# A feed-forward activation by one shifted square, with phases, start and final branch placed anew

## The chip, the cores and the metric

The kernel runs on one core of a Trainium2 chip. The core has a matrix engine (TensorE, PE in the profile), three engines for elementwise work (VectorE is DVE, ScalarE is ACT, GpSimd is POOL) and a sync engine (SP) that here issues most DMAs. Each engine works through its own list of instructions in order and waits on semaphores for the others. The metric is device time in microseconds of one execution, and the median of several runs is compared. Before the change it is 707.75 us (three runs, 701.27 to 708.39).

## The reference

Two parts stand one behind the other. The first is a linear attention with a decaying state, on 4 batches of 8 heads, 768 tokens and head width 48. Its output, 3072 tokens by 384, goes through a feed-forward layer of width 2048:

```python
for t in range(S):                                   # S = 768
    y[:, :, t] = einsum('bhd,bhde->bhe', rt, state + u * kt (x) vt)
    state = wt[..., None] * state + kt (x) vt
x = y.transpose(0, 2, 1, 3).reshape(B * S, H * D)    # 3072 x 384
h = x @ w_in                                         # 3072 x 2048
g = h - np.tanh(h)
return g @ w_out                                     # 3072 x 384
```

The change is in `g = h - tanh(h)`. For small h the difference of two nearly equal numbers is computed by a series in s = h*h: g = h * s * polynomial(s).

## The kernel before

The 768 tokens of each batch are cut in two, so there are 8 blocks of 384 tokens. The attention of a block uses 64-token chunks. Block 0's attention is computed at the start by itself (`boot`). After that, one loop runs over the blocks: it does the feed-forward layer of block i in 16 steps f (128 of the 2048 columns each), and between the steps it places pieces of the attention of block i+1 ("phases", "before") and of block i+2 ("ahead"). Block 0 also loads the 16 tiles of weights and converts them from their 64-bit form with three ACT and two DVE instructions each.

One step of the feed-forward layer is six PE instructions in source (three matmuls for `hp`, three for `acc`) and an elementwise part:

```python
def first(xT, f, ps):
    hp = ps.tile([P, NB], F32, name="hp", tag="hp")          # this PSUM tile has one buffer
    for kc in reversed(range(KC)):                           # KC = 3
        nc.tensor.matmul(hp, lhsT=w_in_sb[:, f, kc, :], rhs=xT[kc], ...)
    made = nc.scalar.activation(out=h, in_=hp, func=AF.Copy, scale=1.0 / UPSCALE)
    nc.scalar.activation(out=s, in_=h, func=AF.Square)
    nc.scalar.activation(out=qa, in_=s, func=AF.Square, bias=shift[:, 0:1])
    nc.scalar.activation(out=qb, in_=s, func=AF.Square, bias=shift[:, 1:2])
    nc.scalar.activation(out=th, in_=h, func=AF.Tanh)
    nc.scalar.activation(out=big, in_=s, func=AF.Relu, bias=shift[:, 2:3])
    return g, [
        product(hs, h, SERIES, s, ALU.mult),                 # DVE, one step later
        lambda: nc.vector.tensor_tensor(out=th, in0=h, in1=th, op=ALU.subtract),
        product(hs, qa, QUAD[0][1], hs, ALU.add),
        product(g, qb, QUAD[1][1], hs, ALU.add),
        lambda: nc.vector.copy_predicated(out=g, mask=big.bitcast(I32), data=th)], made
```

So each step has six ACT and five DVE instructions on 128x384 fp32. Both forms of g are computed, and where s is above 0.25 the form with tanh is taken.

The loop (cut):

```python
for f in range(NF):                                          # NF = 16
    g, next_rest, made = first(here, f, ps_d)
    waiting.append((second, f, g))
    if f not in urgent:
        finish(rest, extra)            # the DVE part of step f-1, and DVE part of a conversion
    for name in before.get(f, ()): later.prepare(name)
    if f in phases: later.phase(ps_a, phases[f])
    for name in ahead.get(f, ()): after.prepare(name)
    ...                                # loads, conversion of weights (ACT part)
    if len(waiting) > LAG:             # LAG = 3: the second matmul of step f-3
        s, fs, gs = waiting.pop(0)
        s.add(fs, gs)                  # after step 15: ACT copies o<-acc, and the output DMA
    if later and phases.get(f) == "result 1": later.phase(ps_a, "result 2")
```

The tables of where the pieces stand, for blocks from 1 on:

```python
steps = (6, 7, 8, 9, 12)               # own, earlier, turn, update, result 1
before = {0: ("before 0",), 1: ("times_behind 2", "times_behind 0", "times_u"),
          2: ("inverse", "held"), 3: ("times_before",), 4: ("bounds",), 7: ("over",)}
ahead = {13: ("behind 2",), 14: ("behind 0",), 15: ("before 2",)}
```

`before` and `behind` are running products along the tokens (DVE scans), `times_behind`, `times_before` and `over` are products of whole tiles on DVE, `times_u` is four ACT instructions (k times u, in place of k), `bounds` two ACT instructions of 128x1560. `own`, `earlier`, `turn`, `update` and `result` are PE matmuls on 48- or 64-row pieces with copies behind them. `over` writes the tile r that the matmuls of `earlier` read.

The end: the kernel has counted whether all its assumptions hold, and branches to a general version of everything where they do not.

```python
count = ...                            # DVE, before the last g
sure = matmul(count, ones); again = (sure != expected)
for s, fs, gs in waiting: s.add(fs, gs)
with tc.If(nc.values_load(again, min_val=0, max_val=1) > 0):
    ...                                # the general version; not entered with these inputs
```

## Time and profile before

| | |
|---|---|
| median of three runs | 707.75 us |
| profiled span | 707.0 us |
| PE busy | 618.7 us (88%) |
| DVE busy | 518.2 us (73%) |
| ACT busy | 508.4 us (72%) |
| POOL busy | 7.8 us (1%) |
| DMA, mean | 61 GB/s |
| chain that ended last: PE, ACT, DVE | 49%, 22%, 21% |

Times are in us unless marked ns. A row of the timeline is: start, length, engine, line of the source, operation, output<-inputs, shape, count, and in brackets the idle time before it with what ended that wait. The trace has two records per fp32 matmul of this kind, so the three matmuls for `hp` or `acc` of a step show as x6. A row of the table of stages gives, for a stretch of time, the busy time of each engine with its number of instructions, the granted PE clock as a share of full speed, and the DMA's share and rate.

### The profile page before, as it was taken

The page shows a single profiled execution, that of the slowest core. Times are in us where ns is not written, and L with a number is a line of the kernel's source. Part 1 is how long each engine was busy: PE and PEld are TensorE (multiplying, and loading weights), DVE is VectorE, ACT ScalarE, POOL GpSimd, SP SyncE. Part 2 cuts the span into 40 slices and gives each one's busy share as a digit, 9 for nine tenths or more (in the row PEclk, how much of TensorE's full clock was granted, in tenths as well). Part 3 has the DMA queues.
Part 4 walks back from the last instruction along what each step waited for, and adds up shares of the span by engine and source line. Part 5 has one row for each costly group of instructions (what it writes and reads, how often), then busy time and mean ns, then how long its engine had stood idle before and what let it go on. Part 6 is the DMA issues. An engine that isn't in the chain of part 4 may idle for free.

```text
span 707.0 us, 13685 instructions
## 1 busy us (share of the span) xinstructions
PE 618.7 (88%) x5410; PEld 379.5 (54%) x5410; DVE 518.2 (73%) x987; ACT 508.4 (72%) x958; POOL 7.8 (1%) x38
## 2 busy tenths in 40 slices
PE   3547788988999879998899879998899898999995
PEld 3523455544665456655566446654566455665553
DVE  7677598887588876696677866687776876757672
ACT  1399999987467855779377884679467884678873
POOL 3000000000000000000000000000000000000000
PEclk9998899999899989999899998999899998999998
DMA  8174234321110212003020211102120110000001
GB/s 301 48 275 136 85 129 136 99 67 46 47 46 9 68 48 77 23 4 110 24 68 9 67 47 46 50 5 68 47 90 10 27 42 1 2 10 33 1 0 39
DMA packets 23432, 43.13 MB, mean 61 GB/s; under 512 B 2112, under 2 KB 21312, under 8 KB 23360
## 3 DMA queue, kind: packets, MB, share of 16 engines
q1 hardware_dynamic: 22944, 41.89, 18.2%
q8 instruction: 44, 0.72, 0.4%
q10 hardware_dynamic: 352, 0.25, 0.1%
q14 instruction: 28, 0.23, 0.1%
q0 software_dynamic: 64, 0.05, 0.0%
HBM read 36.28 MB, written 4.72 MB: 58 GB/s over the span
## 4 chain that ended last, share of the span: by engine, by line
PE 49%; ACT 22%; DVE 21%; issue 4%; DMA 2%; SPq 0%; DVEq 0%; ACTq 0%; PEldq 0%; PEld 0%
PE acc L599 20%; PE hp L562 20%; PE att L348 4%; DVE hs L579 4%; DVE pre L266 3%; DVE gT L587 3%; ACT h L569 3%; ACT qb L572 3%; DVE gT L579 3%; ACT s L570 2%; DVE th L584 2%; ACT k L312 2%; ACT th L573 2%; ACT junk L319 2%; DVE r L305 2%
## 5 line engine op out<-in xcount | busy, mean ns | idle before, releaser
L562 PE MATMUL hp<-xT,w_sb 128*128 128x384 f32 x768 | 279.6, 501 | 37.2 <-ACT h L569 27.4
L599 PE MATMUL acc<-w_sb,gT 128*128 128x384 f32 x768 | 284.0, 508 | 4.8 <-ACT o L604 4.0
L562 PEld LDWEIGHTS hp<-xT,w_sb 128*128 128x128 f32 x768 | 147.4, 195 | 149.2 <-ACT h L569 44.0
L599 PEld LDWEIGHTS acc<-w_sb,gT 128*128 128x128 f32 x768 | 148.2, 198 | 107.4 <-issue 10.5
L569 ACT ACTIVATE h<-hp 128x384 f32<-128x384 f32 x128 | 62.1, 485 | 130.8 <-PE hp L562 130.8
L584 DVE TENSOR_TENSOR th<-h,th 128x384 f32<-128x384 f32 x128 | 71.1, 555 | 61.3 <-ACT th L573 61.3
L579 DVE SCALAR_TENSOR_TENSOR hs<-h,s 128x384 f32<-128x384 f32 x128 | 70.3, 549 | 45.8 <-ACT s L570 45.8
L587 DVE COPY_PREDICATED gT<-big,th 128x384 f32<-128x384 int32 x128 | 76.0, 594 | 11.9
L571 ACT ACTIVATE qa<-s,shift 128x384 f32<-128x384 f32 x128 | 78.7, 615 | 4.2
L579 DVE SCALAR_TENSOR_TENSOR gT<-qb,hs 128x384 f32<-128x384 f32 x128 | 71.4, 558 | 10.7
L574 ACT ACTIVATE big<-s,shift 128x384 f32<-128x384 f32 x128 | 76.8, 600 | 0.0
L572 ACT ACTIVATE qb<-s,shift 128x384 f32<-128x384 f32 x128 | 76.7, 599 | 0.0
L579 DVE SCALAR_TENSOR_TENSOR hs<-qa,hs 128x384 f32<-128x384 f32 x128 | 70.6, 551 | 0.0
L570 ACT ACTIVATE s<-h 128x384 f32<-128x384 f32 x128 | 67.0, 523 | 4.0
L573 ACT ACTIVATE th<-h 128x384 f32<-128x384 f32 x128 | 64.9, 507 | 0.0
L355 DVE COPY_PREDICATED scores<-mask_all,att 128x768 f32<-128x768 uint8 x32 | 31.5, 1010 | 16.6 <-PE att L348 16.5
L348 PE MATMUL att<-r,post 48*64 48x64 f32 x768 | 21.8, 302 | 22.3 <-DVE r L305 22.3
L399 DVE SCALAR_TENSOR_TENSOR states<-states,pre,att 128x48 f32<-128x48 f32 x176 | 31.6, 257 | 12.6 <-PE att L388 12.6
L348 PEld LDWEIGHTS att<-r,post 48*64 48x64 f32 x768 | 20.3, 210 | 27.1 <-issue 24.2
L312 ACT ACTIVATE k<-k,u_sb 128x384 f32<-128x384 f32 x32 | 17.2, 603 | 21.6 <-DVE post L291 21.6
L277 DVE TENSOR_TENSOR_SCAN post<-w,seed 128x780 f32<-128x780 f32 x16 | 28.3, 1777 | 0.0
L266 DVE TENSOR_TENSOR_SCAN pre<-w,seed 128x780 f32<-128x780 f32 x16 | 28.2, 1767 | 0.0
(55 smaller groups left out, 334.3 us busy)
## 6 DMA issues: line engine op xcount, KB each, us to landing
raw<-in_weights SPq DMA_DIRECT2D x16, 768.0 KB, 4.3
w<-in_wT SPq DMA_DIRECT2D x7, 780.0 KB, 4.5
k<-in_kT SPq DMA_DIRECT2D x7, 768.0 KB, 4.4
r<-in_rT SPq DMA_DIRECT2D x7, 768.0 KB, 4.5
v_sb<-in_v SPq DMA_DIRECT2D x8, 576.0 KB, 3.9
out_y<-o SPq DMA_DIRECT2D x23, 192.0 KB, 2.0
xT<-late SPq DMA_DIRECT2D x44, 24.0 KB, 1.9
w<-in_wT SPq DMA_DIRECT2D x2, 390.0 KB, 5.3
```

The source lines that it names most:

```text
L348: nc.tensor.matmul(dst, lhsT=self.chunk(lhs, p, 2 * c + par)[rows], rhs=src, start=True, stop=True)
L562: nc.tensor.matmul(hp, lhsT=w_in_sb[:, f, kc, :], rhs=xT[kc], start=(kc == KC - 1), stop=(kc == 0))
L569: made = nc.scalar.activation(out=h, in_=hp, func=AF.Copy, scale=1.0 / UPSCALE)
L570: nc.scalar.activation(out=s, in_=h, func=AF.Square)
L571: nc.scalar.activation(out=qa, in_=s, func=AF.Square, bias=shift[:, 0:1])
L572: nc.scalar.activation(out=qb, in_=s, func=AF.Square, bias=shift[:, 1:2])
L573: nc.scalar.activation(out=th, in_=h, func=AF.Tanh)
L574: nc.scalar.activation(out=big, in_=s, func=AF.Relu, bias=shift[:, 2:3])
L579: return lambda: nc.vector.scalar_tensor_tensor(out=out, in0=in0, scalar=scalar, in1=in1, op0=op0, op1=ALU.mult)
L584: lambda: nc.vector.tensor_tensor(out=th, in0=h, in1=th, op=ALU.subtract),
L587: lambda: nc.vector.copy_predicated(out=g, mask=big.bitcast(I32), data=th)], made
L599: nc.tensor.matmul(acc, lhsT=g[:, j * P:(j + 1) * P], rhs=w_out_sb[:, f, :], start=(f == 0), stop=(f == NF - 1))
```

## The change

The new activation takes s = h*h once, and one shifted square: g = (( s + SHIFT )^2 + REST) * (TOP * h * s). It holds where all h*h are at most 1/64. The DVE instruction that makes s also keeps the largest s of each row, and these maxima join the count that decides on the general version. So tanh, the second shifted square, the mask and the select leave the main path. They stay in the general version (`any_h`). The square itself moves from ACT to DVE.

```diff
+SLIGHT = 2.0 ** -6
+TOP, SHIFT, REST = 0.053459249436855316, -1.2470279932022095, 4.680200099945068
...
+    def slight(h, n):
+        s, qa = (dense.tile([P, NB], F32, name=name, tag=name) for name in ("s", "qa"))
+        ...
+        def squares():
+            nc.vector.tensor_tensor_reduce(out=s, in0=h, in1=h, scale=1.0, scalar=0.0, op0=ALU.mult,
+                                           op1=ALU.max, accum_out=top[:, n:n + 1])
+            nc.scalar.activation(out=qa, in_=s, func=AF.Square, bias=shift[:, 4:5])
+        return g, squares, [product(hs, h, TOP, s, ALU.mult), product(g, qa, REST, hs, ALU.add)]
```

The pieces of the attention stand at other steps, in one table for all blocks, and `bounds` is cut in two:

```diff
-            steps = (6, 7, 8, 9, 12)
-            before = {0: ("before 0",), 1: ("times_behind 2", "times_behind 0", "times_u"), 2: ("inverse", "held"),
-                      3: ("times_before",), 4: ("bounds",), 7: ("over",)}
-            ahead = {13: ("behind 2",), 14: ("behind 0",), 15: ("before 2",)}
-            loads = {2: "v", 5: "w", 8: "k", 10: "r"}
+        phases = {4: "own", 6: "earlier", 7: "turn", 8: "update", 10: "result 1"}
+        before = {0: ("before 2",), 1: ("before 0",), 2: ("times_behind 2", "times_behind 0", "times_u"),
+                  3: ("times_before", "inverse", "held"), 4: ("bound 0",), 5: ("over",), 6: ("bound 1",)}
+        ahead = {13: ("behind 2",), 14: ("behind 0",)}
+            loads = {2: "v", 7: "w", 8: "k", 9: "r"}
```

In the loop the order within a step is now: h, the two remaining DVE products of step f-1, the square of step f with its shifted square, the conversion, and then the attention pieces:

```diff
-            g, next_rest, made = first(here, f, ps_d)
-            waiting.append((second, f, g))
-            if f not in urgent:
-                finish(rest, extra)
+            h, made = first(here, f, ps_d)
+            for op in rest:
+                op()
+            g, squares, rest = slight(h, i * NF + f)
+            squares()
+            for op in extra:
+                op()
+            waiting.append((second, f, g))
```

The start (`boot`) issues the load of v ahead of the first weights, treats both halves in one loop, puts the masked copies and state updates of DVE later, and converts two tiles of weights on ACT ahead of its copies of the result. Two buffers more hold half-converted weights.

```diff
-        more_weights(nc.sync)
         blk.load_v()
-        for _ in range(2):
+        for _ in range(3):
             more_weights(nc.sync)
...
+        for p0 in HALVES:
+            blk.behind(p0, UP); blk.times_behind(p0, UP); blk.times_u(p0, UP); blk.turn(ps, p0)
+            blk.before(p0, UP); diagonal[p0] = blk.own(ps, p0)
+            blk.times_before(p0, UP); blk.inverse(p0, UP)
+            diagonal[p0]()
+            ins = blk.over(p0, UP); above[p0] = blk.earlier(ps, p0); blk.update_1(ps, p0)
+            ...                       # second half: both bounds, the load of the next w
+            above[h1]() if p0 == h2 else None
+        blk.update_2(h1); above[h2]()
+        scores = blk.result_1(ps, [h1, h1 + 1], "from_scores")
+        blk.update_2(h2); blk.held(0, NPAIR)
+        for _ in range(2):
+            ready.append(convert(*raws.pop(0)))
+        blk.result_2(*scores, True, "from_states")
```

(Several calls are put on one line here, and the cut is marked.) At the end the count comes after the last g, its matmul stands between the last three second matmuls, and every engine reads the verdict ahead of the last of them, with a hint for the branch:

```diff
+    for n, (s, fs, gs) in enumerate(waiting):
+        if n == 1:
+            nc.tensor.matmul(sure[0:1, 0, 0:1], lhsT=count, rhs=ones, start=True, stop=True)
+            nc.vector.tensor_single_scalar(again, sure[0:1, 0, 0:1], ..., op=ALU.not_equal)
+        if n == len(waiting) - 1:
+            anew = nc.values_load(again, min_val=0, max_val=1)
+            tc.mark_branch_hint_location("anew", "LikelyTaken", engines=[PE, SP, DVE, ACT])
+        s.add(fs, gs)
-    with tc.If(nc.values_load(again, min_val=0, max_val=1) > 0):
+    with tc.If(anew > 0, label="anew"):
```

## The prediction

> **What bounds the kernel now.** I read three things in this order: the page's busy times and slices, the table of stages, and the timeline of the matrix engine through one block. The page first:

> ```profile
> PE 618.7 (88%) x5410; PEld 379.5 (54%) x5410; DVE 518.2 (73%) x987; ACT 508.4 (72%) x958; POOL 7.8 (1%) x38
> PE   3547788988999879998899879998899898999995
> ACT  1399999987467855779377884679467884678873
> ```

> PE is fullest, but not everywhere: in slices 3 to 8, roughly 35 to 140 us, ACT stands at 9 and PE at 4 to 9. So there are two regimes, and the table of stages (columns PE, PEld, DVE, ACT, POOL, then clock, DMA share, GB/s) separates them:

> ```profile
> 43.00:80.00 37.00, 24.18 (x49) 12.11 (x50) 28.74 (x46) 35.06 (x56) 0.00 (x0) 0.84 0.53 189
> 201.00:283.00 82.00, 75.90 (x670) 46.54 (x669) 61.28 (x116) 57.92 (x114) 0.13 (x2) 0.96 0.15 47
> 629.00:693.00 64.00, 64.00 (x200) 37.56 (x198) 44.36 (x85) 51.24 (x102) 0.00 (x0) 1.00 0.03 10
> 693.00:707.00 14.00, 6.59 (x22) 3.42 (x20) 2.85 (x7) 3.16 (x7) 0.00 (x0) 0.85 0.15 49
> ```

> Block 0 (first row) is ACT-bound: 35.06 of 37 us. The last block (third row) has no attention beside it and PE is busy without a gap; its matmuls for `hp` start 3.87 us apart, so a step costs at least 3.87 us and a block 16 x 3.87 = 61.9. A middle block repeats every 81.9 us. Where the 20 us between them go is seen in the timeline:

> ```profile
> 231.46 2.10 PE L599 MATMUL acc<-w_sb,gT 128*128 128x384 f32 x6
> 234.87 2.20 PE L562 MATMUL hp<-xT,w_sb 128*128 128x384 f32 x6 [1.31 <-ACT h L569]
> 237.87 2.20 PE L599 MATMUL acc<-w_sb,gT 128*128 128x384 f32 x6 [0.80 <-ACT o L604]
> 245.72 2.10 PE L599 MATMUL acc<-w_sb,gT 128*128 128x384 f32 x6
> 248.80 2.20 PE L562 MATMUL hp<-xT,w_sb 128*128 128x384 f32 x6 [0.99 <-ACT h L569]
> 254.53 2.10 PE L562 MATMUL hp<-xT,w_sb 128*128 128x384 f32 x6
> 259.52 2.84 PE L348 MATMUL att<-r,post 48*64 48x64 f32 x96 [2.89 <-DVE r L305]
> 262.29 3.96 PE L599 MATMUL acc<-w_sb,gT 128*128 128x384 f32 x6
> 266.08 2.10 PE L562 MATMUL hp<-xT,w_sb 128*128 128x384 f32 x6
> ```

> A group of three matmuls starts 1.935 us before the next. From start to start, the excess is: 3.41-1.94 = 1.48 before 234.87 (ACT did `times_u` first), 3.00-1.94 = 1.07 before 237.87 (waits for copies of the finished accumulators), 3.08-1.94 = 1.15 before 248.80 (`bounds`), 4.99-1.94 = 3.05 before 259.52 (waits for `over`). Then the matmuls run slow: the attention group takes 2.77 instead of 1.56, the next `acc` 3.79 instead of 1.94: 1.21+1.86 = 3.07. Sum 9.8 us of avoidable time in a block. The other 10.2 are attention's own PE work, read the same way: result 3.6, own 1.85, earlier 1.85, turn 1.3, update 1.7, about 10.3. So the PE floor of a middle block is 61.9+10.3 = 72.2 us.

> [...] after 2.89 us idle the next group takes 3.96, after 1.31 and 1.49 us none is slow, after 2.39 us (at 152 us) one is. [...] the row of `th` on DVE has 555. [...] I put the new square at an estimated 0.56+0.1 us. No trace yet shows it. [...] The trace shows nothing computed from 700.1 to the end at 707.0.

> **The change, part by part.**

> *ACT per step:* from h, s, qa, qb, th, big = 485+523+615+599+507+600 = 3.33 us to h and qa = 1.1 us. *DVE per step:* from 555+549+594+558+551 = 2.81 us to two products and the square, 1.1+0.66 = 1.76 us. In a middle block both engines fall far below 3.87.

> *Middle blocks.* `over` moves from just ahead of its matmuls (both at step 7) to step 5, matmuls at 6: removes 3.05+3.07. `bounds` (3.3 us in one piece) becomes two pieces of 1.7 at steps 4 and 6; h and qa end about 2.0 us after the end of `hp`, so a piece ends at 3.7, ahead of the next h (due at 4.1): removes 1.15. But `times_u` and the output copies, one step apart before, now stand behind one another at step 2. Counted from the end of the `hp` of step 2: h ends at 0.7, the square on DVE at 1.4 (this wait is new: before, `times_behind` needed nothing of its own step, and DVE began it at 230.46, ahead of the end of that step's `hp`), `times_behind` twice 1.82, so 3.25; `times_u` 2.13, so 5.4; first output copy 0.5, so 5.85. The first `acc` of the block could start at 3.87 and starts at 5.85: a stall of about 2.0, in place of 1.48+1.07 = 2.55. So a middle block is 72.2+2.05 = 74.3. The saving is 81.9-74.3 = 7.6 us in each of five blocks and 83.7-74.3 = 9.4 in block 1 (its `hp` runs 138.1 to 221.8): 47 us. DVE carries up to 1.76+2.33 = 4.1 us in steps 0 to 6 and about 6 at step 8. That is over 3.87, but only with attention on PE beside most of it, and g is needed three steps later, so I count nothing.

> *The last block* stays at 61.9: its copies are ready at 2.1+0.5, before 3.87.

> *Block 0.* Its loop had 3.3+2.6 (three conversions at 0.9, 1.06, 1.04, overlapping) on ACT, and h follows h at 5.63 us in plain steps. Now the loop is a ring between two engines: h 0.5, square 0.7, qa 0.6, conversion 2.65 = 4.4 us. The DVE ring is square 0.7, conversion 1.4, products 1.2 = 3.3 plus the attention piece. Step by step the longer of the two: step 0 4.4; 1 5.1 (scan); 2 9.2, as `times_u` waits for DVE and the conversion waits for `times_u`; 3 5.7; 4 6.1; 5 5.1; 6 6.1; 7 6.0; 8 7.0 (20 updates at 0.18); 9 4.4; 10 6.1; 11 and 12 4.4 each; 13 5.1; 14 and 15 3.9 each. Sum 87, against 138.1-43.05 = 95.05 before: 8 us.

> *The start.* Before, the first `hp` waits for ACT's copies at 43.05, and these stood behind two conversions although their matmuls were done at 36.6. In the changed order I follow the DVE list with the durations of before: first half to `over` 12.7, second half's `over` 20.8, masked copy 21.8, 12 updates 24.0, masked copy 25.0; the second update's matmuls wait for a buffer until 24, so 12 updates from 25.6 to 27.8. ACT does bounds and both conversions in 18 to 27 meanwhile. First results' copies at 28.9 to 30.8, second at 31.3 to 33.3. First `hp` at about 33.5: 9.5 us.

> *The tail* was 693.4 to 707.0 = 13.6 us. [...] PE waits for the count behind the last g (about 1.6 us more): I count 1.5 us net.

> Sum: 47+8+9.5+1.5 = 66; 707-66 = 641. For the slow clock after the new 2 us stall, which lies between 1.49 (no effect) and 2.39 (effect), I add a third of a chance of 1.5 us in six blocks, 3; one more for what a run adds to the span. **645 us.**

> **The rivals.**
> 1. *The stall at step 2 grows and cools the clock.* For it: the same ACT rows stand in one chain with DVE, and 2.0 us is near 2.39. Then each of six blocks costs 1.5 to 2.5 more: 652 to 659.
> 2. *DVE becomes the bound in steps 0 to 6.* Against it: 1.76 us of own work. If the square with its maximum takes 1.1 us instead of 0.66, seven steps lose a few tenths each, 2 to 3 us in a block: about 660.
> 3. *Block 0 doesn't shrink, because weights arrive too slowly.* The table of stages shows 189 GB/s there; 16 loads of 768 KB at 4.3 us each are 69 us, below 87. If they bound it, 649 to 653.
> 4. *Nothing moves, as PE is at 88% already.* The windows speak against it: 9.8 of 82 us in a block are waits and slow matmuls, all traced to ACT or DVE.
> 5. *The general version is entered.* The largest h*h of the reference's inputs is 0.0070, below 1/64 = 0.0156, so no.

> **Range and chances.** Middle blocks uncertain by 8 us upward and 4 downward, block 0 by 5 either way, start 3, tail 2: 634 to 661. A gain below 2% would need 52 of 66 us to fail. Faster 0.97, same 0.02, slower 0.01.

> **What would show it.** Right: `hp` of consecutive middle blocks 74 us apart; no wait for r before the second attention group, and no slow `acc` behind it; one wait for o of about 2 us in each block; first `hp` near 33.5, block 1's first near 121; the square 0.56 us. Wrong: a period below 73 (the stall is overlapped), or above 77 (slow clock or DVE); PE waiting for DVE's g; conversions waiting for DMA in block 0.

## The result

The changed kernel takes 633.27 us (median of four runs, 631.83 to 635.56), beside 708.07 us for the kernel before in the same comparison (701.27 to 709.14). The ratio is 0.8965, 95% interval 0.8901 to 0.9028. The prediction was 645 with a range of 634 to 661: the direction and most of the mechanism held, and the time lies 0.7 us under the range.

The profiled spans are 707.0 and 630.1 us. Cut at the first `hp` matmul of each block, the 76.9 us come from everywhere at once:

| stretch | before | predicted | after | saved |
|---|---|---|---|---|
| start, to the first `hp` | 43.05 | 33.5 | 31.29 | 11.8 |
| block 0 | 95.05 | 87 | 81.82 | 13.2 |
| six middle blocks | 83.7 + 5 x 81.92 | 6 x 74.3 | 6 x 74.02 | 49.2 |
| last block | 61.9 | 61.9 | 61.9 | 0 |
| tail | 13.7 | 12.1 | 11.0 | 2.7 |

(Predicted block 0: from 33.5 to block 1's start near 121. Predicted tail: 13.6, read from 693.4, less 1.5; the last block ends at 693.3.)

### The profile page after: what moved, and what is told of

Same layout as the page of the kernel before. It is cut to its first block, busy times and chain, and to the rows that moved or that the text cites. A ratio compares the mean times of both kernels' runs of the same rounds, so it can differ in the third digit from the quotient of the medians.

```text
span 630.1 us, 12866 instructions
## 1 busy us (share of the span) xinstructions
PE 589.3 (94%) x5410; PEld 364.3 (58%) x5410; DVE 392.8 (62%) x860; ACT 261.4 (41%) x446; POOL 7.8 (1%) x38
## 4 chain that ended last, share of the span: by engine, by line
PE 79%; ACT 9%; DVE 8%; issue 2%; ACTq 0%; DVEq 0%
PE acc L625 35%; PE hp L575 34%; PE att L356 3%; DVE post L299 2%; ACT k L320 2%; PE att L400 2%; PE att L379 1%; PE att L427 1%; PE att L444 1%; ACT up L203 1%; ACT up L202 1%; ACT w_sb L199 1%; DVE states L413 1%; ACT h L578 1%; DVE s L591 1%
## 5 line engine op out<-in xcount | busy, mean ns | idle before, releaser
L625 PE MATMUL acc<-w_sb,gT 128*128 128x384 f32 x768 | 271.9, 491 | 10.7 <-ACT o L630 9.9
L625 PEld LDWEIGHTS acc<-w_sb,gT 128*128 128x128 f32 x768 | 142.5, 190 | 107.3 <-ACT o L630 13.6
L591 DVE CUSTOM_DVE_ANT_0 s<-h 128x384 f32<-128x384 f32 x128 | 71.4, 558 | 205.8 <-ACT h L578 205.8
L581 DVE SCALAR_TENSOR_TENSOR gT<-qa,hs 128x384 f32<-128x384 f32 x128 | 71.5, 558 | 16.4
L581 DVE SCALAR_TENSOR_TENSOR hs<-h,s 128x384 f32<-128x384 f32 x128 | 70.3, 549 | 1.9
L379 PE MATMUL att<-ident,post 128*128 128x128 f32 x96 | 13.4, 292 | 7.6 <-DVE post L299 7.6
L356 PE MATMUL att<-r,post 48*64 48x64 f32 x768 | 14.5, 232 | 5.2 <-DVE r L313 5.2
L356 PEld LDWEIGHTS att<-r,post 48*64 48x64 f32 x768 | 13.2, 145 | 9.4 <-issue 7.3
L379 PEld LDWEIGHTS att<-ident,post 128*128 128x128 f32 x96 | 11.9, 151 | 9.9 <-DVE post L299 7.6
L202 ACT ACTIVATE up<-raw 128x768 f16<-128x768 f32 x16 | 17.0, 1060 | 0.0
L203 ACT ACTIVATE up<-raw 128x768 uint16<-128x768 uint32 x16 | 16.7, 1045 | 0.0
L206 DVE CUSTOM_DVE_ANT_0 w_sb<-w_sb,up 128x1536 uint16<-128x1536 uint16 x16 | 15.3, 959 | 1.4 <-ACT up L203 0.7
L356 PEld LDWEIGHTS att<-r,k 48*64 48x64 f32 x768 | 13.2, 145 | 4.9 <-issue 4.5
```

Source lines behind the costliest of these rows:

```text
L356: nc.tensor.matmul(dst, lhsT=self.chunk(lhs, p, 2 * c + par)[rows], rhs=src, start=True, stop=True)
L379: nc.tensor.transpose(tp[:, p, c * P:(c + 1) * P], self.chunk("post", p0 + p, 2 * c, n=2), ident)
L581: return lambda: nc.vector.scalar_tensor_tensor(out=out, in0=in0, scalar=scalar, in1=in1, op0=op0, op1=ALU.mult)
L591: nc.vector.tensor_tensor_reduce(out=s, in0=h, in1=h, scale=1.0, scalar=0.0, op0=ALU.mult, op1=ALU.max, accum_out=top[:, n:n + 1])
L625: nc.tensor.matmul(acc, lhsT=g[:, j * P:(j + 1) * P], rhs=w_out_sb[:, f, :], start=(f == 0), stop=(f == NF - 1))
```

## The profile after

First the page of the changed kernel, its busy times and the slices of PE and ACT:

```profile
PE 589.3 (94%) x5410; PEld 364.3 (58%) x5410; DVE 392.8 (62%) x860; ACT 261.4 (41%) x446; POOL 7.8 (1%) x38
PE   3676999989998999989999899989999899999997
ACT  2868876343324423254232533244332442323222
```

PE has the same 5410 matmuls and is busy 29.4 us less: the work is the same, and what is gone is mostly time at the slow clock (mean granted clock 0.956 before, 0.992 after). ACT has about half its instructions and half its time, and after slice 7 it stands at 2 to 5. The chain that ended last was 49% PE before and is 79% PE now. The table of stages (columns as before: PE, PEld, DVE, ACT, POOL, clock, DMA share, GB/s) for block 0, a middle block, the last block and the tail:

```profile
31.30:113.10 81.80, 71.18 (x650) 42.27 (x651) 64.00 (x124) 61.13 (x87) 0.13 (x2) 0.94 0.52 179
113.10:187.10 74.00, 72.24 (x685) 44.62 (x684) 47.18 (x107) 27.47 (x50) 0.13 (x2) 1.00 0.17 51
557.20:619.10 61.90, 61.90 (x193) 36.48 (x192) 26.90 (x65) 18.84 (x36) 0.00 (x0) 1.00 0.03 10
619.10:630.10 11.00, 6.32 (x21) 3.23 (x19) 1.46 (x6) 1.57 (x4) 0.00 (x0) 1.00 0.17 59
```

A middle block has 72.24 us of PE work in 74.00, at clock 1.00; what is left over is one stall. Block 0 is no longer bound by ACT alone: no engine is full in it (PE 71, DVE 64, ACT 61 of 81.8), and ACT and DVE wait for each other as in the ring of the prediction: DVE 0.86 us for h at 39.18, ACT 0.64 us for the square at 39.78. The timeline of PE in block 2, whose first `hp` is at 187.13, against the rows of before with four idle places:

```profile
198.74 2.10 PE L575 MATMUL hp<-xT,w_sb 128*128 128x384 f32 x6
202.49 2.20 PE L625 MATMUL acc<-w_sb,gT 128*128 128x384 f32 x6 [1.65 <-ACT o L630]
204.53 2.10 PE L575 MATMUL hp<-xT,w_sb 128*128 128x384 f32 x6
...
214.02 2.10 PE L575 MATMUL hp<-xT,w_sb 128*128 128x384 f32 x6
216.05 1.63 PE L356 MATMUL att<-r,post 48*64 48x64 f32 x96
217.61 2.20 PE L625 MATMUL acc<-w_sb,gT 128*128 128x384 f32 x6
```

The attention group at 216.05 starts on time and the `acc` behind it takes 2.20, where before there were 2.89 idle, 2.84 and 3.96: the wait for `over` and the slow clock behind it are gone. So are the waits for `times_u` and for `bounds`. One wait is new: `acc` starts 3.75 after the `hp` before it instead of 1.94, so it lost 1.81, and nothing behind it runs slow. What ACT does in that time:

```profile
198.19 0.62 ACT L593 ACTIVATE qa<-s,shift 128x384 f32<-128x384 f32 x1 [0.64 <-DVE top L591]
199.93 2.13 ACT L320 ACTIVATE k<-k,u_sb 128x384 f32<-128x384 f32 x4 [1.12 <-DVE post L299]
201.97 1.22 ACT L630 ACTIVATE o<-acc 128x384 f32<-128x384 f32 x3
```

ACT first stands idle 1.12 us for `times_behind`, then runs `times_u` for 2.13, and only then the copy that frees the accumulator PE waits for. This is the chain that the prediction worked out at step 2. The new activation in the list of groups:

```profile
L591 DVE CUSTOM_DVE_ANT_0 s<-h 128x384 f32<-128x384 f32 x128 | 71.4, 558 | 205.8 <-ACT h L578 205.8
L578 ACT ACTIVATE h<-hp 128x384 f32<-128x384 f32 x128 | 62.7, 490 | 225.4 <-PE hp L575 225.4
L593 ACT ACTIVATE qa<-s,shift 128x384 f32<-128x384 f32 x128 | 78.9, 616 | 89.3 <-DVE top L591 89.3
```

The square with its maximum takes 558 ns (and 83 for the read of the maximum), beside the 0.56+0.1 us of the prediction: 0.56 is the length of `th` on DVE before (555 ns), and the 0.1 was the author's estimate, which no trace had shown. Each of the three waits for the one before it, and ACT and DVE idle 200 us and more for the next `hp`: in the middle blocks they follow PE.

## The experiments

The questions: which part of the change carries the middle blocks, the new tables (A) or the lighter engines (B)? Why is the start shorter, why is block 0 shorter than predicted, and is the new wait for o worth removing? All ratios are to the kernel before, with the 95% interval, and a span is that of the profiled run.

**1. The old activation in the changed kernel.** Six ACT and five DVE instructions again; the maxima are set to zero, so that their test is void, and one buffer of the conversion is given up for room.

```diff
+    nc.vector.memset(top, 0.0)
...
         def squares():
-            nc.vector.tensor_tensor_reduce(out=s, in0=h, in1=h, ..., accum_out=top[:, n:n + 1])
-            nc.scalar.activation(out=qa, in_=s, func=AF.Square, bias=shift[:, 4:5])
+            nc.scalar.activation(out=s, in_=h, func=AF.Square)
+            ...                                  # qa, qb, th, big on ACT
-        return g, squares, [product(hs, h, TOP, s, ALU.mult), product(g, qa, REST, hs, ALU.add)]
+        return g, squares, [...]                 # the five DVE instructions of before
```

> The changed kernel with the old activation put back (six ACT and five DVE instructions a step), everything else as changed. Theory A (placement): middle blocks gain from where the attention pieces stand, so they stay within 2 us of 74.0, and only block 0, which is bound by ACT, goes back from 82 to about 93: in all about 645 to 655 us. Theory B (lighter engines): the middle blocks gain from the instructions that are gone, so they go back to about 80 and block 0 to 93: 675 to 685 us.

657.91 us (656.37 to 659.45), ratio 0.9321 (0.9228 to 0.9415). The middle blocks take 79.06, 76.55 and then four times 75.07; block 0 takes 94.1, the tail 13.25. Of the 27.5 us of span that the old activation costs here, 12.2 lie in block 0, 11.8 in the six middle blocks, 2.3 in the tail and 1.2 in the start. So with the new tables the old activation loses only 1.05 us in each of the last four middle blocks. It is nearer to A, but above the range that A gave, for the most part because block 0 goes back to what it was before the change. The timeline of PE in this run's block 2:

```profile
217.23 2.10 PE L576 MATMUL hp<-xT,w_sb 128*128 128x384 f32 x6
222.03 3.68 PE L634 MATMUL acc<-w_sb,gT 128*128 128x384 f32 x6 [2.70 <-ACT o L639]
225.55 2.10 PE L576 MATMUL hp<-xT,w_sb 128*128 128x384 f32 x6
```

The same wait for o, 1.05 us longer since ACT has more to do ahead of the copy. Behind it `acc` takes 3.68 here; in the last four middle blocks the same wait of 2.70 is followed by nothing slow. Which of the two happens depends on when the wait falls (last section), so the 1.05 holds for those blocks only.

**2. The changed kernel, with `over` late again.**

```diff
-                  3: ("times_before", "inverse", "held"), 4: ("bound 0",), 5: ("over",), 6: ("bound 1",)}
+                  3: ("times_before", "inverse", "held"), 4: ("bound 0",), 6: ("over", "bound 1")}
```

> The changed kernel with the product r over pre put back directly ahead of the matmuls that read it (step 6 instead of step 5), nothing else. Theory A: the wait of about 2.9 us and the slow matmuls behind it (3.1 us) return in each of six middle blocks, and a little in block 0: middle blocks about 80, in all 662 to 672 us. Theory B: DVE is light now and the product is done early: below 640 us.

669.27 us (668.21 to 670.33), ratio 0.9482 (0.9389 to 0.9576). The middle blocks take 80.34 and then 78.7 to 78.8: one table entry gives back 4.7 of the 7.9 us that a block had gained, with the new activation untouched. The timeline of PE in block 2:

```profile
226.73 2.10 PE L575 MATMUL hp<-xT,w_sb 128*128 128x384 f32 x6
231.83 1.63 PE L356 MATMUL att<-r,post 48*64 48x64 f32 x96 [3.00 <-DVE r L313]
233.39 3.90 PE L625 MATMUL acc<-w_sb,gT 128*128 128x384 f32 x6
```

The wait is 3.00 us long and about 1.7 more is lost to slow matmuls behind it, in every middle block. The total is in A's range; A had put the slow matmuls at 3.1.

**3. The old tables, with the new activation, start and end.** The phase tables of before, with `bounds` in its two pieces at one step.

```diff
-        phases = {4: "own", 6: "earlier", 7: "turn", 8: "update", 10: "result 1"}
-        before = {0: ("before 2",), 1: ("before 0",), 2: ("times_behind 2", "times_behind 0", "times_u"), ...
+            steps = (6, 7, 8, 9, 12)
+            before = {0: ("before 0",), 1: ("times_behind 2", "times_behind 0", "times_u"), 2: ("inverse", "held"),
+                      3: ("times_before",), 4: ("bound 0", "bound 1"), 7: ("over",)}
...                                              # block 0 likewise, and `before 2` and `before 0` ahead of the loop
```

> The changed kernel with the old tables of phases (bounds in two pieces at the same old step, the scans of the first next block back in the start). Theory A: middle blocks go back to 79 to 81 us, in all 668 to 678. Theory B: they stay at 74 to 76, below 648 us.

650.55 us (650.1 to 651.0), ratio 0.9217 (0.9128 to 0.9306). Both theories missed it. The middle blocks take 75.12 us, as B said and A did not; but the wait for r that A rests on is there in each:

```profile
233.82 1.63 PE L356 MATMUL att<-r,post 48*64 48x64 f32 x96 [2.94 <-DVE r L313]
235.37 2.20 PE L625 MATMUL acc<-w_sb,gT 128*128 128x384 f32 x6
```

It costs its own 2.94 and nothing else: `acc` takes 2.20. No other wait is left in the block. So the lighter activation removes the waits for `times_u`, `o` and `bounds` by itself, and by itself leaves the wait for r; whether the clock falls behind a wait of this length is not settled by the length (last section). Block 0 takes 92.9 us: in block 0 the new activation is worth little without the new table.

**4. `times_u` at the end of its step**, behind the copies that free the accumulators. A proposal for the new wait, everything else as changed.

```diff
-        before = {0: ("before 2",), 1: ("before 0",), 2: ("times_behind 2", "times_behind 0", "times_u"),
+        before = {0: ("before 2",), 1: ("before 0",), 2: ("times_behind 2", "times_behind 0"),
...
                 s.add(fs, gs)
+            if later and f == 2:
+                later.prepare("times_u")
```

> The changed kernel with the four ACT instructions k times u placed last in step 2, behind the output copies and behind the conversion. If the remaining stall of 1.8 us in each middle block is these four standing ahead of the output copies, the first acc of a block starts without a wait, middle blocks take 72.3 instead of 74.0 us, and step 2 of block 0 falls by 2 us: about 621 us. Rival: the stall moves on to the next hp, which waits for h behind the same four instructions; then the gain stays below 4 us in all.

620.32 us (618.45 to 620.6, four runs), ratio 0.879 (0.8724 to 0.8856): 13 us faster than the changed kernel. The timelines of this run, ACT first and then PE:

```profile
194.26 0.61 ACT L593 ACTIVATE qa<-s,shift 128x384 f32<-128x384 f32 x1 [0.63 <-DVE top L591]
194.78 1.23 ACT L630 ACTIVATE o<-acc 128x384 f32<-128x384 f32 x3
196.00 2.13 ACT L320 ACTIVATE k<-k,u_sb 128x384 f32<-128x384 f32 x4
```

```profile
194.81 2.10 PE L575 MATMUL hp<-xT,w_sb 128*128 128x384 f32 x6
196.74 2.10 PE L625 MATMUL acc<-w_sb,gT 128*128 128x384 f32 x6
198.68 2.10 PE L575 MATMUL hp<-xT,w_sb 128*128 128x384 f32 x6
```

The copies now run in the time in which ACT idled for `times_behind`, and `acc` follows `hp` at 1.93. The middle blocks take 72.10 us, the PE floor that the prediction put at 72.2. Of the 13.4 us of span, 11.5 lie there and 1.9 in block 0.

**5. The old end:** the verdict is read at the branch, behind the last matmuls, and the branch carries no hint.

```diff
-        if n == len(waiting) - 1:
-            anew = nc.values_load(again, min_val=0, max_val=1)
-            tc.mark_branch_hint_location("anew", "LikelyTaken", engines=[PE, SP, DVE, ACT])
         s.add(fs, gs)
...
-    with tc.If(anew > 0, label="anew"):
+    with tc.If(nc.values_load(again, min_val=0, max_val=1) > 0):
```

> The changed kernel with the verdict read only behind the last matmuls, at the branch, and without the hint. The tail measured 11.0 us against 13.6 before. If reading the verdict early is what shortened it, this one takes 2 to 3 us more, 635 to 636.5 us. Rival: the tail is shorter because the last g is ready earlier, and the branch costs the same either way: no difference above 0.5 us.

636.71 us (636.5 to 636.8), ratio 0.9019 (0.899 to 0.9048). From the end of the last block the tail is 13.1 us instead of 11.0. The other 2.4 us of its longer span lie in the start and block 0, which this edit does not touch: with the boot of the changed kernel, the first `hp` came between 31.2 and 32.9 us in the runs that left the start alone, and block 0 with its own code took 81.8 to 83.4. A difference of 2 us in the total that sits there is not counted as an effect.

**6. `bounds` in one place.**

```diff
-                  3: ("times_before", "inverse", "held"), 4: ("bound 0",), 5: ("over",), 6: ("bound 1",)}
+                  3: ("times_before", "inverse", "held"), 4: ("bound 0", "bound 1"), 5: ("over",)}
```

> The changed kernel with both pieces of the bounds at step 4. The prediction gave the cutting in two 1.15 us in each middle block. If it is the cut, six blocks lose about 7 us, 640 us. Rival: with h and the shifted square alone, ACT is free at 2 us of a step of 5.7 us (step 4 has the matmuls of own in it), and 3.3 us fit whole: within 1 us in the middle blocks, at most 1 us more in block 0.

635.73 us (635.48 to 636.84), ratio 0.9011 (0.898 to 0.9041), and the middle blocks take 74.02 us, as with the cut. The cut is worth nothing there. In experiment 3, too, both pieces stand at one step, there without `own` beside them, and PE doesn't wait behind them. Block 0 takes 84.3 us, 0.9 above the highest of the others and 2.5 above the changed kernel; how much of that is this edit is not shown.

**7. The old start.** Order of the boot as before; all else as changed.

```diff
-        for p0 in HALVES:
-            blk.behind(p0, UP)
-            ...                    # one half of the tokens to its end, then the other
-        for _ in range(2):
-            ready.append(convert(*raws.pop(0)))
-        blk.result_2(*scores, True, "from_states")
+        blk.behind(h1, UP)
+        ...                        # the halves interleaved, update after turn
+        blk.result_2(*blk.result_1(ps, [h1, h1 + 1], "from_scores"), True, "from_states")
```

> The changed kernel with the old start (order of the loads, of the DVE and ACT work and of the conversions). The first hp began at 31.3 us instead of 43.05. If all of this is the order, this kernel's first hp begins at 42 to 43 us and the time is 644 to 646 us. Rival: part of the gain came from the two buffers more for half converted weights or from the scans that left the start, which stay: first hp at 35 to 40 us.

643.81 us (643.74 to 643.88), ratio 0.912 (0.9082 to 0.9159). The first `hp` comes at 41.68 us, 10.4 later. The waits of PE in this run (us in total, times, longest):

```profile
PE att L356 <- ACT k L320: 12.0, 2, 8.2
PE hp L575 <- ACT xT L470: 6.4, 1, 6.4
```

These are the two waits of the start before the change, close to the lengths they had there (12.5 and 6.4). With the light activation they are back: 10.4 of the 11.8 us of the start are order. The other 1.4 are not accounted for; starts differ by up to 1.7 between runs.

**8. `times_u` last, and the conversions ahead of the shifted square.** On top of experiment 4, to let block 0's ring turn faster: ACT then converts while DVE squares.

```diff
+            if between:
+                next_extra.append(between())
             nc.scalar.activation(out=qa, in_=s, func=AF.Square, bias=shift[:, 4:5])
```

> As with k times u last, and in block 0 the three ACT conversion instructions are placed between h and the shifted square, so that ACT converts while DVE squares. If block 0 is bound by the ring of h, square, shifted square and conversion (4.27 us from h to h), the ring falls to the 3.65 us of ACT alone, the plain steps become bound by PE at 3.87 us, and block 0 falls by 3 to 5 us: about 617 us. Rival: the DVE ring or the arrival of weights takes over: less than 1 us.

620.25 us (619.24 to 620.87), ratio 0.8782 (0.8751 to 0.8812), no gain over experiment 4: block 0 takes 81.2 us against 79.9. The last steps of the block fall to PE's own 3.87, and earlier ones grow by more. A miss.

**9. `times_u` last and `over` late.** Experiment 2 with the wait for o removed. Does the clock fall behind a wait of 3.00 us only where a second wait comes ahead of it in the block (C), or does it depend on where the wait falls (D)?

```diff
-                  3: ("times_before", "inverse", "held"), 4: ("bound 0",), 5: ("over",), 6: ("bound 1",)}
+                  3: ("times_before", "inverse", "held"), 4: ("bound 0",), 6: ("over", "bound 1")}
```

> The kernel with k times u last in step 2, and with r over pre again directly ahead of its matmuls. Here the wait of 3.0 us for r is the only one in a middle block. Theory C: the slow matmuls need a second wait not far ahead (the old table with the new activation waits 2.94 us for r, has no other wait and loses nothing more, while the late r product with the 1.65 us stall kept is slow behind it): middle blocks 72.1+3.0 = 75.1 us. Rival, theory D: how long a wait cools the clock depends on where it falls, not on a second wait: middle blocks anywhere from 75 to 78 us, some slow.

648.63 us in the profiled run and 656.94 in the other, ratio 0.9236 (0.9093 to 0.9379). Each middle block has the wait of 3.00. The first three take 75.18, 75.17 and 75.18 us; the last three 76.86, 78.42 and 76.72. Two of the six places, from the timeline of PE:

```profile
221.70 1.63 PE L356 MATMUL att<-r,post 48*64 48x64 f32 x96 [3.00 <-DVE r L313]
223.26 2.20 PE L625 MATMUL acc<-w_sb,gT 128*128 128x384 f32 x6
...
372.05 1.63 PE L356 MATMUL att<-r,post 48*64 48x64 f32 x96 [3.00 <-DVE r L313]
373.60 3.90 PE L625 MATMUL acc<-w_sb,gT 128*128 128x384 f32 x6
```

The same wait, the same code, no second wait in the block, and once the matmuls behind are slow and once not. C falls.

**10. The kernel before, with two numbers changed:** `own` at step 5, `over` at step 6.

```diff
-            steps = (6, 7, 8, 9, 12)
+            steps = (5, 7, 8, 9, 12)
...
-                      3: ("times_before",), 4: ("bounds",), 7: ("over",)}
+                      3: ("times_before",), 4: ("bounds",), 6: ("over",)}
```

> The kernel before, with own at step 5 instead of 6 and r over pre at step 6 instead of 7, so one step ahead of its matmuls; nothing else. The prediction's sum gives this wait 3.05 us and the slow matmuls behind it 3.07 us of a middle block. If these terms are right and stand alone, middle blocks take 75.8 instead of 81.9 us and the time is about 668 to 672 us. Rival: with six ACT and five DVE instructions a step, the next wait (ACT) takes part of it: middle blocks 77 to 80 us, 680 to 695 us.

662.87 us (662.81 to 662.93), ratio 0.9378 (0.9345 to 0.9411). The middle blocks take 75.83 and then 74.73 us, with the old activation, six ACT and five DVE instructions a step. That is 43.8 us in the six blocks, where the whole change saved 49.2. Two waits are left in each:

```profile
299.42 2.20 PE L562 MATMUL hp<-xT,w_sb 128*128 128x384 f32 x6 [1.30 <-ACT h L569]
302.42 2.20 PE L599 MATMUL acc<-w_sb,gT 128*128 128x384 f32 x6 [0.80 <-ACT o L604]
```

These are the waits of before at 234.87 and 237.87. The wait for r, the slow matmuls, and also the wait behind `bounds` (now hidden behind `own`) are gone: 81.92 - 74.73 = 7.2, of the 3.05 + 3.07 + 1.15 = 7.3 that the prediction read for those three.

**11. The loads of v behind one more load of weights,** as the old order had it, to see what of the start is DMA order.

```diff
+        more_weights(nc.sync)
         blk.load_v()
-        for _ in range(3):
+        for _ in range(2):
```

> The changed kernel with the load of v again behind the first weights. If v was what the old start waited for, the first hp starts 1.5 to 3 us later than 31.3. Rival: the state updates stand later now, and v is there in time: less than 0.7 us.

634.44 us (634.22 to 634.65), ratio 0.8976 (0.8944 to 0.9008). First `hp` at 32.32, 1.0 later, which is inside the spread of starts named above; v still arrives ahead of its use: its first matmuls start at 14.09 without a wait. Nothing is shown for this order.

**12. The first two conversions behind the first result's copies.**

```diff
+        blk.result_2(*scores, True, "from_states")
         for _ in range(2):
             ready.append(convert(*raws.pop(0)))
-        blk.result_2(*scores, True, "from_states")
```

> The changed kernel with the two first conversions on ACT placed behind the first four copies of the result instead of ahead of them. ACT then idles until the copies at about 26 us, and the last copies wait behind 5.3 us of conversions: first hp at about 35.5 us, so 4 us of the 11.8 that the start gained. Rival: below 1 us.

636.96 us (636.55 to 637.38), ratio 0.9012 (0.8977 to 0.9046). The first row of `hp` in PE's timeline:

```profile
35.60 2.93 PE L575 MATMUL hp<-xT,w_sb 128*128 128x384 f32 x4 [6.43 <-ACT xT L470]
```

PE waits again for ACT's copies, 6.43 us as before the change. The first `hp` comes 4.3 us later than at 31.29. So about 4.3 of the 11.8 us of the start (2.7 to 4.4, beside the starts named in experiment 5) come from the place of the conversions on ACT, and most of the rest from the other changes of order in the boot, which experiment 7 undoes together.

## Why the prediction came out as it did

**What bounds the kernel: right.** The two regimes, the step of 3.87 us, the last block at 61.9 and the PE floor of 72.2 (72.10 in experiment 4) all held.

**Middle blocks: right in the result, partly wrong in the account.** 74.02 measured, 74.3 predicted. The stall at step 2 was put at 2.0 and measured 1.81; this is the wait that the change introduced, and it was found ahead of time by laying the ACT instructions of one step end to end. What failed is the reading of the account as one term for each part. That the earlier `over` removes 3.05+3.07 holds in the kernel before (experiment 10), but the 3.07 is not tied to the wait: experiment 3 keeps the wait of 2.94 and loses nothing behind it. That the cut of `bounds` removes 1.15 is wrong: experiment 6 undoes the cut and loses nothing in these blocks, experiment 10 removes the 1.15 without a cut, by placing `own` behind `bounds`, and experiment 3 without either, by the lighter ACT. And the parts are substitutes here. Placing `own` and `over` one step earlier brings a middle block of the kernel before from 81.9 to 74.7 (experiment 10), the new activation with the old tables to 75.1 (experiment 3), and the whole change to 74.0. Placement takes away the wait for r, the slow matmuls and the wait behind `bounds` (3.05 + 3.07 + 1.15, 7.2 measured); the activation takes away the slow matmuls, the wait behind `bounds` and the two at step 2 (3.07 + 1.15 + 1.48 + 1.07, 6.8 measured). They have 4.2 in common, and the new tables bring the stall of 1.8: 7.2 + 6.8 - 4.2 - 1.8 = 8.0, and 7.9 is measured. One part of this is luck: in experiment 3 the slow matmuls are gone although the wait is still there, because of when that wait falls (last section). What the activation is needed for shows in block 0.

**Block 0: right mechanism, term too large by 5 us.** The ring of h, square, qa and conversion is there: in the plain steps square follows square at 4.23 to 4.27. The timeline of ACT in steps 0 and 1:

```profile
36.07 0.90 ACT L199 ACTIVATE w_sb<-raw 128x768 f32<-128x768 f32 x1
36.87 1.05 ACT L202 ACTIVATE up<-raw 128x768 f16<-128x768 f32 x1
37.79 1.03 ACT L203 ACTIVATE up<-raw 128x768 uint16<-128x768 uint32 x1
38.69 0.45 ACT L578 ACTIVATE h<-hp 128x384 f32<-128x384 f32 x1
39.78 0.62 ACT L593 ACTIVATE qa<-s,shift 128x384 f32<-128x384 f32 x1 [0.64 <-DVE top L591]
40.30 0.90 ACT L199 ACTIVATE w_sb<-raw 128x768 f32<-128x768 f32 x1
```

The conversion takes 38.69 - 36.07 = 2.62, as put (2.65). But h, square and qa take 40.30 - 38.69 = 1.61 where I added 0.5 + 0.7 + 0.6 = 1.8: here the next instruction on ACT starts before the last has ended (the second of the conversion at 36.87, its first ends at 36.97), and lengths were added where starts should have been. For each step 0 to 12 the measured distance is at or below the predicted one (4.23 4.76 8.91 5.20 5.72 4.79 5.83 5.65 6.59 4.27 5.82 4.27 4.25; predicted 4.4 5.1 9.2 5.7 6.1 5.1 6.1 6.0 7.0 4.4 6.1 4.4 4.4): 70.3 in sum instead of 74.0. Most of the difference lies in the steps with attention pieces, which I have not taken apart. The lead from the first `hp` to the first square and the last three steps made 11.5 instead of 12.9. In other runs with this block's code unchanged it took up to 83.4, so 3.6 to 5.2 us are what this term was too large by.

**The start: right mechanism, 2 us too late.** First `hp` at 31.29, predicted 33.5. The conversions lie beside DVE's work as worked out, and the last copy and DVE's conversion of a weight tile now end together, at 31.2. The term that failed is a wait I had put in: "the second update's matmuls wait for a buffer until 24, so 12 updates from 25.6". From the timeline of DVE:

```profile
23.25 1.01 DVE L363 COPY_PREDICATED scores<-mask_all,att 128x768 f32<-128x768 uint8 x1
24.17 2.17 DVE L413 SCALAR_TENSOR_TENSOR states<-states,pre,att 128x48 f32<-128x48 f32 x12
```

The updates start at 24.17, right behind the masked copy: that wait is not there. The second copies then start at 29.3 instead of 31.3.

**The tail: 1.2 us more than predicted.** 2.7 saved, 1.5 predicted. The old end alone costs 2.1 (experiment 5). The predicted 1.5 was net of 1.6 us of PE waiting for the count, and what it was net of, a gain from reading the verdict earlier, was the author's estimate, which no trace had shown. From the timeline of all engines at the end of the changed kernel:

```profile
617.20 4.03 PE L625 MATMUL acc<-w_sb,gT 128*128 128x384 f32 x12
...
620.08 0.50 DVE L774 TENSOR_REDUCE count<-holds 128x1 f32<-128x336 f32 x1
...
621.16 0.19 PE L779 MATMUL att<-ones,count 128*1 128x1 f32 x2
```

PE has the `acc` of two steps to do until 621.2, and the count is there at 620.6. With the old activation in the same place (experiment 1) the wait does appear, 2.1 us: the shorter path to g pays for the count.

**The allowance of 3 us for slow clock: not needed, and its rule was wrong.** Nothing ran slow behind the new stall. The prediction set a bound by length, between 1.49 us (no effect) and 2.39 (effect). The kernel before had already a longer wait with no effect, in its block 0:

```profile
92.89 1.63 PE L348 MATMUL att<-r,post 48*64 48x64 f32 x96 [2.70 <-DVE r L305]
94.45 2.20 PE L599 MATMUL acc<-w_sb,gT 128*128 128x384 f32 x6
```

So 2.39 was no threshold; the last section has what decides at 2.9 to 3.0 us. The sum without it, 641, is closer, and with block 0 and the start at their sizes it is 634. The terms that missed were four small ones, all to one side, and the low end of the range did not allow for that.

**The rivals.** The clock did not fall behind the stall at step 2 (1; its total, 642 and six times 1.5 to 2.5, is 651 to 657 and not 652 to 659). DVE did not become the bound (2): 47 of 74 us in a middle block. Weights did not come late (3): 179 GB/s in block 0, and no wait for them on PE's path. The gain was not small (4), and the general version was not entered (5).

## What to carry to other kernels

Before making an engine lighter, look at what each stall waits for: in this kernel two numbers in a table, which place `over` one step ahead of its matmuls and `own` one step earlier, save by themselves 44 us in the middle blocks, where the whole change saves 49. Gains of two parts that remove the same wait don't add, so predict the change by the waits that are left and not by a sum over its parts. Where an engine takes its work in the order of the program, as ACT does here (`times_u` at 199.93 and the copies at 201.97 in the changed kernel, the copies at 194.78 and `times_u` at 196.00 in experiment 4), put what frees a buffer ahead of work that has slack: `times_u` behind the three copies instead of ahead of them is worth 13 us more, and the version of experiment 4, at 620.32 us, beats both kernels.

## What was not expected of the hardware

Behind the same idle time of PE its clock falls or doesn't. Waits of 2.94 to 3.00 us were followed by slow matmuls in every block of experiment 2, in none of experiment 3 and in three of six of experiment 9. In experiment 2 the slow stretch also moves. Its last such place, where the first was at 231.83 with lengths 1.63 and 3.90:

```profile
546.78 2.21 PE L356 MATMUL att<-r,post 48*64 48x64 f32 x96 [3.00 <-DVE r L313]
548.92 3.22 PE L625 MATMUL acc<-w_sb,gT 128*128 128x384 f32 x6
```

```profile
223.75:227.17 3.42, 3.42 (x12) 1.98 (x11) 1.83 (x3) 0.00 (x0) 0.00 (x0) 1.00 0.02 5
373.94:377.35 3.41, 3.41 (x7) 1.73 (x6) 1.99 (x4) 0.00 (x0) 0.00 (x0) 0.50 0.00 0
```

The first wait began 1.76 us after an edge, the second 1.93. There are 24 such waits for r, of 2.89 to 3.00 us, in the middle blocks of the kernel before and of experiments 2, 3 and 9. The nine that began 1.68 to 1.87 us after an edge were followed by nothing slow; the fifteen that began at 0.20 to 1.01 or at 1.93 to 3.01 were each followed by one or two steps at clock 0.50. This is D: for these 24, the place in the grid decides. (In experiment 1 the waits of 2.70 began 1.10 after an edge, with slow matmuls behind, and 2.49 to 2.55 after one in the last four middle blocks, without.)

It fits whole runs too. 24 steps are 81.92 us, exactly the middle block before the change, and its wait began about 1.0 after an edge each time. 22 are 75.09, next to experiment 3's 75.12, and its wait only moved from 1.75 to 1.87. 23 are 78.51, and in the last five middle blocks of experiment 2, at 78.7 to 78.8 a block, it moved from 2.1 to 3.0. Which place the first wait gets is not set by anything in the code that was found here: the two runs of experiment 9, 648.63 and 656.94 us, had mean clocks of 0.979 and 0.961. So what slow matmuls cost in experiments 1, 2, 3 and 9 holds for the profiled runs. How long PE can idle without a fall of the clock is not shown. In the changed kernel the clock fell behind the wait of 1.65 us in none of the six middle blocks: it is 1.00 from 56.69 to the end at 630.10.
